# Attention and mixture of experts in one kernel: pooled value sums split 80 + 64 instead of 128 + 16, and two steps of the last slot issued earlier

## The chip, the cores and the metric

The kernel runs on one core of a Trainium2 chip. Its time is the device time of one execution in microseconds (us). The times shown are three runs and one execution under the hardware profiler.

## The reference

What is computed is attention at two scales, added up, and its rows then go through a mixture of eight experts, of which each row uses one:

```python
B, H, S, D = 8, 8, 576, 64
# q, k, v pooled: means over 4 neighbouring tokens, 144 rows in all
q_d, k_d, v_d = (t.reshape(B, H, S // 4, 4, D).mean(axis=3) for t in (q, k, v))
out_up = np.repeat(softmax(q_d @ k_d.T / 8) @ v_d, 4, axis=2)
mask = np.abs(pos[:, None] - pos[None, :]) < 4
out_local = softmax(where(mask, q @ k.T / 8, -1e9)) @ v
x = (out_up + out_local), as [4608 rows, 512]
# mixture of experts: E = 8, w1 [E, 512, 1024], w2 [E, 1024, 512]
logits = normalized(x) @ normalized(expert_emb).T / tau
e = argmax(logits)
out[row] = softmax(logits)[e] * (relu(x[row] @ w1[e]) @ w2[e])
```

## The kernel before

**Attention stage.** A unit is one batch and one pair of heads: 32 units, `for i in range(-2, n + 1)` in `attention`. The order of the operations in one round of that loop is written out by hand in `ORDER`, and `LEAD` says how many units ahead of the round each operation works. The operations that concern the change are those of the pooled attention, on 144 pooled tokens, which are cut into two pieces by the constant `CD` (line 26), because 144 is more than the 128 partitions:

- `load_v` (line 345) loads the values of one unit, one pooled token (four rows of 64 numbers, for each of two heads) in a partition. Piece 0 is one DMA, piece 1 another, both issued by SyncE (SP) into one tile `ld_v` (program name `vr`), of which there are three. `load_v(u + 3)` is called once `vd` of unit u is issued.
- `op_pv` (line 407) adds, on GpSimd (POOL), two rows of each four to the other two, once for each piece. `op_vd` (line 411) adds the two sums that are left, for both pieces in one instruction over all partitions of the tile; the rows of piece 1 that hold no token were set to zero at the start (line 246).
- `op_wdT` (line 493) transposes the pooled attention weights `ad` on TensorE (PE), three transposes for each piece, `op_adT` (line 499) copies them out of PSUM on ScalarE (ACT), and `op_vald` (line 505) multiplies them with `vd`: for each piece and head one fp32 matmul, which the trace shows as two passes. The pieces are accumulated in PSUM.

**Slot stage.** The rows are sorted by expert into slots of at most 128 rows. Three slots are handled early, 38 in `run_slots` (line 1007), and five more by a second call of `run_slots` in `last_slots` (line 1088), inside an `If` whose flag says whether there are that many; in the data used here the flag is zero and the block is skipped. For a slot q, `mm1_half` multiplies with w1 (twice 12 matmuls), `hidden_high` and `hidden_low` split the result into two fp16 parts, `hidden_T` transposes them by DMA into `hT`, and `mm2_part` multiplies with w2 (24 matmuls), which in the program's order is done one slot later, while slot q + 1 is at its first product. `out_rows` scales the result on ACT, and `store` scatters it to DRAM by an indirect DMA of POOL. The last slot has no successor: its second product, `self.mm2(last)` on line 1079, stands alone at the end.

The weights on chip belong to one expert. `renew(which, b)` (line 992) holds the steps that replace them when the expert changes, inside `If`s on a code which ACT, VectorE (DVE) and POOL have in a register. When the `If` isn't taken, the engine branches over it and then, at the line of the `If` (995), waits for its own earlier instructions and raises its semaphore by as much as the block would have. TensorE waits for these semaphores before it reads w2.

In `run_slots` the steps at the end of a slot are issued in this order: `weigh` (ACT exponential, line 1184), `out_rows(q - 1)` (ACT, line 1259), a conditional load, `gate` (DVE), `renew(1, b)`, `store(q - 1)` (POOL, line 1263). The value of the flag for the rare slots is read by `values_load` (line 1091), which puts a number into a register of each of the five engines; the branch on it is line 1092. The end of the program is line 1394.

Of the kernel before, what the change touches and what calls it, by code (L numbers as in the profile page):

```python
# [8 lines left out]
F32 = mybir.dt.float32  # L9
# [10 lines left out]
B, H, S, D = 8, 8, 576, 64  # L20
N, DM, E, FF = B * S, H * D, 8, 1024
NHP = H // 2
SD = S // 4
G, QB = S // 64, 32
WK, WV = QB + 6, 64 + 6
CD = (128, SD - 128)
CP = S // 6
TB = 128
NTB = -(-S // TB)
# [3 lines left out]
NEARLY, BEARLY = 3, B - 2  # L33
AHEAD = 4
NFIX = NSLOT - 5
# [27 lines left out]
class Kern:  # L63
# [128 lines left out]
    def attention(self, ctx):  # L192

        nc = self.nc
# [3 lines left out]
        z = self.pool(ctx, "zeroed", 1)  # L198
        self.kq, self.an, self.qdbd, self.vw, self.xT, self.sums = [], [], [], [], [], []
        for i in range(2):  # L200
# [3 lines left out]
            self.an.append(z.tile([128, G, WV], F32, name=f"an{i}"))  # L204
            self.sums.append(z.tile([128, G + 3], F32, name=f"sums{i}"))
            self.vw.append(z.tile([WV, G, 4, D], F32, name=f"vw{i}"))
        self.vr = [z.tile([128, 2, 2, 4 * D], F32, name=f"ld_v{i}") for i in range(3)]
        self.lg = z.tile([TB, NTB, E + 1], F32, name="lg")
        self.oh = self.cp.tile([TB, B, NTB + 1, E], BF16, name="oh")
        units = [(b, hp) for b in range(B) for hp in range(NHP)]  # L210
# [32 lines left out]
            nc.vector.memset(self.xT[i][:, S:], 0.0)  # L243
            nc.vector.memset(self.sums[i], 1.0)
        for vr in self.vr:
            nc.gpsimd.memset(vr[:, 1], 0.0)
        next(crows)
        load(1)
        load_v(0)
# [12 lines left out]
        for i in range(-2, n + 1):  # L262
# [4 lines left out]
            for j, (name, args) in enumerate(ops):  # L267
# [10 lines left out]
                else:  # L278
# [6 lines left out]
                    s = st[u]  # L285
# [31 lines left out]
            if i >= 1 and units[i - 1][1] == NHP - 1:  # L317
                for f in tail:
                    f()
                b = units[i - 1][0]  # L320
# [88 lines left out]
        self.nc.gpsimd.tensor_tensor(out=vr[:, :, 0:2 * D], in0=vr[:, :, 0:2 * D], in1=vr[:, :, 2 * D:], op=ALU.add)  # L409

    def op_vd(self, s):
        v, vd = s["v"], self.wk.tile([128, 2, 2, D], F32, name="vd")
        s["vd"] = vd
        self.nc.gpsimd.tensor_tensor(out=vd, in0=v[:, :, :, 0:D], in1=v[:, :, :, D:2 * D], op=ALU.add)

# [82 lines left out]

    def op_adT(self, s, c):
        if "adT" not in s:  # L500
            s["adT"] = self.wk.tile([128, 2, 2, 3, 48], F32, name="adT", bufs=1)
        self.nc.scalar.activation(out=s["adT"][:CD[c], c].rearrange("p h c j -> p c h j"),
                                  in_=s["wdT", c].rearrange("p c (h j) -> p c h j", h=2), func=AF.Copy)

# [499 lines left out]
        with tc.If(code > 4 if which else code < 1):  # L1004
            self.measure(which)

    def run_slots(self, q0, q1):

        last = q1 - 1
        for q in range(q0, q1):  # L1010
            b = q - NEARLY
            old, new, ahead = q > q0, q < last, q + 2 < q1
            first = self.mm1_half(q, 0)
            self.total(slice(0, 2))
            second = self.mm1_half(q, 1)
            if old:
                self.scale_gate(q - 1)
            self.scales(slice(0, 2))
            h2 = self.hidden_high(first)
            self.hidden_low(first, h2)  # L1020
            if not b:
                self.flags(1)
            self.nc.vector.tensor_copy(out=self.wcur, in_=self.wold)
            if new:
                self.renew(0, b + 1)
            if ahead:
                self.x_square(q + 2)
            h3 = self.hidden_high(second)
            if new:
                self.measure_staged(0, b + 1)  # L1030
            if ahead:
                self.x_power(q + 2)
            if b:
                self.measure_staged(1, b)
            ps, done = None, 0
            if old or not b:
                ps, done = (None, 0) if b else (self.begun, 4)
                ps = self.mm2_part(q - 1, done, done + 1, ps)
                done += 1
            if not b:  # L1040
                for _ in self.late:
                    pass
            if ahead:
                self.x_high(q + 2)
            if b + 2 < q1 - NEARLY:
                self.flags(b + 2)
            self.logits(q, False)
            self.hidden_T(q, 0, h2)
            if q + 4 < q1:
                self.gather(q + 4)  # L1050
            if ps:
                self.mm2_part(q - 1, done, 4 if b else 6, ps)
            if new:
                self.stage_next(0, b + 1, 0)
            self.hidden_low(second, h3)
            if ps:
                self.mm2_part(q - 1, 4 if b else 6, 8, ps)
            self.hidden_T(q, 1, h3)
            if ahead:
                self.x_low(q + 2)  # L1060
            self.weigh(q)
            if ahead:
                self.turn(q + 2)
            if ps:
                self.out_rows(q - 1, ps)
            if q > q0 + 1:
                self.stage_next(1, b - 1, 1)
            self.gate(q)
            if old:
                self.renew(1, b)  # L1070
            if new:
                self.norms(q + 1)
                self.stage_next(0, b + 1, 1)
            if ps:
                self.store(q - 1)
            if old:
                self.stage_next(1, b, *((0,) if new else (0, 1)))
        self.scale_gate(last)
        self.mm2(last)
        self.store(last)  # L1080

# [6 lines left out]
    def last_slots(self):  # L1088

        q0, q1 = NEARLY + NFIX, NEARLY + NSLOT  # L1090
        more = self.nc.values_load(self.flg[:1, NFIX, 3:4], min_val=0, max_val=1)  # L1091
        with self.tc.If(more > 0):
            for q in range(q0, min(q0 + 4, q1)):
                self.gather(q)
            for b in (NFIX, NFIX + 1):
                self.flags(b)
            self.rescale()
            for w in range(2):
                self.renew(w, NFIX)
                if not w:  # L1100
                    self.nc.vector.tensor_copy(out=self.wcur, in_=self.wold)
                    self.measure_staged(0, NFIX)
                self.stage_next(w, NFIX, 0, 1)
            self.open_slots(q0)
            self.run_slots(q0, q1)
# [161 lines left out]
    def run(self):  # L1267
        tc, ctx = self.tc, self.ctx
        ctx.enter_context(tc.manual_schedule())
        self.bk = self.pool(ctx, "banks", 8, space=PSUM)  # L1270
        self.cp = self.pool(ctx, "const", 1)
        self.dr = self.pool(ctx, "scratch", 1, space=DRAM)
        self.weight_tiles()
        self.slot_pools()
        n = B * NHP
        with ExitStack() as actx:
            w0 = self.first_weights()
            steps = self.attention(actx)
            early = self.early_slots()
            for at in steps:  # L1280
                if at is None:
                    break
                if at in EARLY:
                    next(early)
                i, end = at
                if end and i in W0:
                    next(w0, None)
                if at == (n - 1, 1):
                    ps = [self.mm1_half(0, 0, 0, 1)]
                if at == (n, 1):  # L1290
                    self.mm1_half(0, 0, 1, 3, ps[0])

            next(steps)
            self.mm1_half(0, 0, 3, 4, ps[0])
            ps.append(self.mm1_half(0, 1, 0, 2))
            next(steps)
            for _ in steps:
                pass
        self.hd = self.pool(ctx, "hidden", 2)
        self.hidden(0, 0, ps[0])  # L1300
        self.mm1_half(0, 1, 2, 4, ps[1])
        self.sw = self.pool(ctx, "slots", 1)
        slots = self.slots()
        next(slots)
        self.hidden(0, 1, ps[1])
        w1 = self.second_weights()
        for _ in range(2):
            next(w1)
        next(slots)
        self.hidden(1, 0, self.mm1_half(1, 0))  # L1310
        next(w1)
        self.hidden(1, 1, self.mm1_half(1, 1))
        next(w1)
        ps = self.mm1_half(2, 0)
        next(slots)
        self.gather(NEARLY)
        self.hidden(2, 0, ps)
        next(w1)
        self.gates(0)
        for q in range(1, AHEAD):  # L1320
            self.gather(NEARLY + q)
        ps = self.mm2_part(0)
        self.out_rows(0, ps)
        self.store(0)
        self.x_size(NEARLY)
        ps = self.mm1_half(2, 1)
        self.x_split(NEARLY)
        self.hidden(2, 1, ps)
        next(w1)
        self.gates(1)  # L1330
        self.x_size(NEARLY + 1)
        self.norms(NEARLY)
        ps = self.mm2_part(1)
        self.x_split(NEARLY + 1)
        next(w1)
        self.out_rows(1, ps)
        self.store(1)
        next(slots)
        self.begun = self.mm2_part(2, 0, 4)
        self.gates(2)  # L1340
        for _ in range(3):
            next(w1)
        for _ in self.slot_flags():
            pass

        def late():
            next(slots)
            yield from w1

        self.late = late()  # L1350
        self.run_slots(NEARLY, NEARLY + NFIX)
        self.last_slots()


# [43 lines left out]
```

## Time and profile before

| | us |
|---|---|
| three runs | 730.84, 736.08, 740.85 |
| their median | 736.08 |
| the profiled execution | 733.08 |
| its span, first to last instruction | 731.4 |
| busy in it: PE, DVE, ACT, POOL | 701.0, 473.1, 462.0, 443.4 |

The profiled execution is one of the faster ones. Its span ends 1.7 us short of its own time. Durations and instants below are counted from the start of that span. In the profile, a row of a group has the line, engine, operation, names, shapes and count, then total busy time and the mean in ns of one, then idle time before it and what ended that idle time.

### The profile page before, as it was taken

The numbers are of one execution on the slowest core, as the hardware profiler recorded it, in microseconds if no ns is written. First come the engines' busy times: TensorE is split into PE (matmuls) and PEld (weight loads), VectorE is DVE, ScalarE is ACT, GpSimd is POOL, SyncE is SP. The second block draws the span as 40 slices with busy tenths as digits, with TensorE's granted clock in tenths as the row PEclk, the third lists the DMA queues.
The fourth block names the chain that finished last, engine by engine and source line by source line (L and its number), as shares of the span: only waits on it lengthen the run. The fifth ranks groups of instructions, "written<-read, shape, count | busy, mean of one in ns | idle before, by whom it ended". The sixth has DMA issues, their size and how long they took to land. (4 is left out here: it accounts for less than half of the span.)

```text
span 731.4 us, 22049 instructions
## 1 busy us (share of the span) xinstructions
PE 701.0 (96%) x7471; PEld 412.9 (56%) x7471; DVE 473.1 (65%) x1415; ACT 462.0 (63%) x1063; POOL 443.4 (61%) x857
## 2 busy tenths in 40 slices
PE   8999999989999989999999999999999999999992
PEld 5777887768878864444444444444444444444440
DVE  6778799958998887576556467565643565366320
ACT  4677788667787664356666577775755555558420
POOL 5865788765878885556564564556466645564420
PEclk9999999989999999999999999999999999999997
DMA  9889889988788976959959988898897599779640
GB/s 162 163 202 193 221 185 234 211 210 213 158 215 185 215 244 129 221 123 248 235 126 250 231 208 216 191 247 193 251 220 132 116 238 216 147 175 202 177 74 19
DMA packets 284117, 138.92 MB, mean 190 GB/s; under 512 B 251186, under 2 KB 260402, under 8 KB 283968
## 3 DMA queue, kind: packets, MB, share of 16 engines
q1 hardware_dynamic: 277248, 118.15, 73.8%
q0 software_dynamic: 6560, 19.03, 8.2%
q8 instruction: 61, 1.00, 0.6%
q14 instruction: 88, 0.72, 0.3%
q10 hardware_dynamic: 160, 0.02, 0.0%
HBM read 213.05 MB, written 20.33 MB: 319 GB/s over the span
## 5 line engine op out<-in xcount | busy, mean ns | idle before, releaser
L1214 PE MATMUL bank<-w1h,xT 128*128 128x512 f16 x328 | 124.3, 379 | 1.4 <-ACTq L995 1.4
L1250 PE MATMUL bank<-w2h,hT 128*128 128x512 f16 x328 | 124.4, 379 | 0.9 <-ACTq L995 0.9
L1215 PE MATMUL bank<-w1l,xT 128*128 128x512 f16 x328 | 124.3, 379 | 0.1
L1252 PE MATMUL bank<-w2h,hT 128*128 128x512 f16 x328 | 124.4, 379 | 0.0
L1251 PE MATMUL bank<-w2l,hT 128*128 128x512 f16 x328 | 124.4, 379 | 0.0
L1216 PE MATMUL bank<-w1h,xT 128*128 128x512 f16 x328 | 124.3, 379 | 0.0
L1111 POOL DMA_INDIRECT xg<-xd,ids x41 | 45.8, 1118 | 79.7 <-POOLq L995 36.9
L1227 ACT ACTIVATE h<-bank 128x512 f16<-128x512 f32 x82 | 48.3, 589 | 58.4 <-PE bank L1216 57.5
L1263 POOL DMA_INDIRECT out_dram<-o,ids x41 | 44.9, 1096 | 50.0 <-ACTq L995 20.0
L380 ACT ACTIVATE kq<-bank 128x288 f32<-128x288 f32 x128 | 48.1, 472 | 38.8 <-PE bank L373 38.4
L833 ACT ACTIVATE junk<-st 128x1024 bf16<-128x1024 f32 (+1 forms) x30 | 67.5, 2251 | 4.6 <-DVE end L734 2.7
L1259 ACT ACTIVATE o<-bank,gt 128x512 f32<-128x512 f32 x41 | 27.8, 677 | 63.5 <-issue 18.7
L409 POOL TENSOR_TENSOR ld_v<-ld_v 128x256 f32<-128x256 f32 x64 | 48.9, 783 | 22.6 <-DMA ld_v<-in_v_dram 22.6
L389 POOL TENSOR_TENSOR pool_kq<-kq 128x288 f32<-128x288 f32 x62 | 45.3, 731 | 25.1 <-ACT kq L380 25.1
L81 POOL TENSOR_SCALAR nw_t<-nw_y,nw_a 128x1 f32<-128x1 f32 x123 | 51.7, 420 | 12.4
L1231 DVE SCALAR_TENSOR_TENSOR h<-bank,h 128x512 f16<-128x512 f32 x82 | 56.3, 688 | 2.7 <-ACTq L1004 2.2
L858 DVE SCALAR_TENSOR_TENSOR w2l<-st,wscl,w2h 128x1024 f16<-128x1024 f32 x32 | 39.6, 1280 | 26.1 <-ACT w2h L857 26.1
L1214 PEld LDWEIGHTS <-xT 128*128 128x128 f16 x328 | 35.1, 107 | 34.5 <-DMA xT<-x 0.5
L1251 PEld LDWEIGHTS <-hT 128*128 128x128 f16 x328 | 32.0, 98 | 39.4 <-issue 1.2
L1250 PEld LDWEIGHTS <-hT 128*128 128x128 f16 x328 | 32.0, 98 | 39.0 <-DMA hT<-h 0.6
L1216 PEld LDWEIGHTS <-xT 128*128 128x128 f16 x328 | 31.9, 97 | 39.1 <-issue 0.4
L1252 PEld LDWEIGHTS <-hT 128*128 128x128 f16 x328 | 32.0, 98 | 38.8
(221 smaller groups left out, 1556.2 us busy)
## 6 DMA issues: line engine op xcount, KB each, us to landing
st<-in_moe_w_dram SPq DMA_DIRECT2D x148, 1024.0 KB
ld_k<-in_k_dram SPq DMA_DIRECT2D x64, 144.0 KB
ld_q<-in_q_dram SPq DMA_DIRECT2D x64, 144.0 KB
xd<-xr SPq DMA_DIRECT2D x8, 1040.0 KB
ld_v<-in_v_dram SPq DMA_DIRECT2D x32, 256.0 KB
st<-in_moe_w_dram SPq DMA_DIRECT2D x16, 512.0 KB
vw<-in_v_dram SPq DMA_DIRECT2D x64, 122.5 KB
vw<-in_v_dram SPq DMA_DIRECT2D x32, 64.0 KB
```

The source lines that it names most:

```text
L81: g.tensor_scalar(out=t, in0=y, scalar1=y, scalar2=a, op0=ALU.mult, op1=ALU.mult)
L380: self.nc.scalar.activation(out=dst, in_=s["qk", r, w].rearrange("p (m i) -> p i m", m=3), func=AF.Copy, scale=(KSC, QSC)[w])
L409: self.nc.gpsimd.tensor_tensor(out=vr[:, :, 0:2 * D], in0=vr[:, :, 0:2 * D], in1=vr[:, :, 2 * D:], op=ALU.add)
L833: self.nc.scalar.activation(out=junk, in_=src, func=AF.Square, accum_out=acc)
L1214: nc.tensor.matmul(out=ps, lhsT=xT[:, 0, k], rhs=self.w1h[:, k, ns], start=(k == 0), stop=False)
L1215: nc.tensor.matmul(out=ps, lhsT=xT[:, 0, k], rhs=self.w1l[:, k, ns], start=False, stop=False)
L1216: nc.tensor.matmul(out=ps, lhsT=xT[:, 1, k], rhs=self.w1h[:, k, ns], start=False, stop=(k == self.KC - 1))
L1227: self.nc.scalar.activation(out=h2[:, 0], in_=ps, func=AF.Relu)
L1231: self.nc.vector.scalar_tensor_tensor(out=h2[:, 1], in0=ps, scalar=0.0, in1=h2[:, 0], op0=ALU.max, op1=ALU.subtract)
L1250: nc.tensor.matmul(out=ps, lhsT=hh, rhs=self.w2h[:, j, :], start=(j == 0), stop=False)
L1251: nc.tensor.matmul(out=ps, lhsT=hh, rhs=self.w2l[:, j, :], start=False, stop=False)
L1252: nc.tensor.matmul(out=ps, lhsT=hl, rhs=self.w2h[:, j, :], start=False, stop=(j == self.FC - 1))
```

## The change

`CD` goes from (128, 16) to (80, 64), and the tiles `ld_v`, `vd` and `adT` from 128 partitions to 80. The zeros at the start are written only to rows 64 to 79 of piece 1. In `run_slots`, the renewal of w2 for the last slot stands ahead of `out_rows(q - 1)`, a conditional load and `gate` rather than behind them; for all other slots it stays. The load of the rare slots' flag is issued after `scale_gate(last)`, ahead of `mm2(last)`, instead of after `store(last)`; the `If` on it stays where it was.

```diff
-CD = (128, SD - 128)
+CD = (80, SD - 80)
...
-        self.vr = [z.tile([128, 2, 2, 4 * D], F32, name=f"ld_v{i}") for i in range(3)]
+        self.vr = [z.tile([CD[0], 2, 2, 4 * D], F32, name=f"ld_v{i}") for i in range(3)]
...
-            nc.gpsimd.memset(vr[:, 1], 0.0)
+            nc.gpsimd.memset(vr[CD[1]:, 1], 0.0)
...
-        v, vd = s["v"], self.wk.tile([128, 2, 2, D], F32, name="vd")
+        v, vd = s["v"], self.wk.tile([CD[0], 2, 2, D], F32, name="vd")
...
-            s["adT"] = self.wk.tile([128, 2, 2, 3, 48], F32, name="adT", bufs=1)
+            s["adT"] = self.wk.tile([CD[0], 2, 2, 3, 48], F32, name="adT", bufs=1)
...
-    def run_slots(self, q0, q1):
+    def run_slots(self, q0, q1, end=None):
...
             self.weigh(q)
             if ahead:
                 self.turn(q + 2)
+            if old and not new:
+                self.renew(1, b)
             if ps:
                 self.out_rows(q - 1, ps)
             if q > q0 + 1:
                 self.stage_next(1, b - 1, 1)
             self.gate(q)
-            if old:
+            if old and new:
                 self.renew(1, b)
...
         self.scale_gate(last)
+        if end:
+            end()
         self.mm2(last)
         self.store(last)
...
-        more = self.nc.values_load(self.flg[:1, NFIX, 3:4], min_val=0, max_val=1)
-        with self.tc.If(more > 0):
+        with self.tc.If(self.more > 0):
...
-        self.run_slots(NEARLY, NEARLY + NFIX)
+
+        def more():
+            self.more = self.nc.values_load(self.flg[:1, NFIX, 3:4], min_val=0, max_val=1)
+
+        self.run_slots(NEARLY, NEARLY + NFIX, more)
```

## The prediction, made before the changed kernel was run

> **What bounds the kernel now.** First the page's head, then the windows of the two stages and of the one stretch that stands out, to see whether TensorE ever has room.
>
> ```profile
> span 731.4 us, 22049 instructions
> PE 701.0 (96%) x7471; PEld 412.9 (56%) x7471; DVE 473.1 (65%) x1415; ACT 462.0 (63%) x1063; POOL 443.4 (61%) x857
> ...
> 17.00:275.00 258.00, 249.01 (x5166) 198.69 (x5166) 215.04 (x550) 193.39 (x623) 193.27 (x312) 0.99 0.87 203
> 145.00:153.00 8.00, 5.78 (x121) 4.33 (x119) 5.42 (x16) 7.39 (x23) 5.68 (x10) 1.00 1.04 282
> 153.00:161.00 8.00, 7.48 (x128) 6.45 (x128) 3.26 (x7) 3.16 (x7) 3.28 (x6) 0.57 0.65 161
> ```
>
> A windows row gives the length, then busy us of PE, weight loads, DVE, ACT and POOL, the granted clock, the DMA engines' busy share and GB/s. PE is busy 249 of the attention stage's 258 us: it bounds that stage, and the other engines have a quarter of it free. The DMA engines, at 0.87, are the second bound, and the first in bursts: in 145 to 153 they are full and PE idles 2.2 of 8 us, and in the next 8 us its clock is granted at 0.57, so some 0.43 x 8 = 3.4 us more are lost. What the changed operations wait for in that stage, by the view of waits:
>
> ```profile
> POOL ld_v L409 <- DMA ld_v<-in_v_dram: 22.6, 10, 5.0
> PE bank L522 <- DMA vw<-in_v_dram: 3.3, 5, 2.0
> PE bank L509 <- POOL vd L414: 0.9, 1, 0.9
> ```
>
> The pooled values' loads make POOL wait ten times, 22.6 us in all, but POOL has that time: PE waited only once, 0.9 us, for `vd`. Next the end, by the timeline:
>
> ```profile
> 707.05 0.19 ACT L1184 ACTIVATION_READ_ACCUMULATOR lg<-lg,lmx 128x1 f32 x1
> 710.84 0.38 PE L1252 MATMUL bank<-w2h,hT 128*128 128x512 f16 x1
> 711.30 0.69 ACT L1259 ACTIVATE o<-bank,gt 128x512 f32<-128x512 f32 x1 [4.07 <-issue]
> 712.09 0.38 PE L1250 MATMUL bank<-w2h,hT 128*128 128x512 f16 x1 [0.87 <-ACTq L995]
> ...
> 716.83 0.38 PE L1251 MATMUL bank<-w2l,hT 128*128 128x512 f16 x1
> 717.05 0.38 PE L1252 MATMUL bank<-w2h,hT 128*128 128x512 f16 x1
> 717.60 0.69 ACT L1259 ACTIVATE o<-bank,gt 128x512 f32<-128x512 f32 x1 [5.61 <-PE bank L1252]
> 718.57 0.99 POOL L1263 DMA_INDIRECT out_dram<-o,ids  x1 [5.07 <-ACT o L1259]
> ```
>
> At 712.09 the last second product starts late, and L995, the `If` of `renew`, is what it waited for. Matmuls follow each other by 0.22 us (716.83, 717.05), so the lateness is 712.09 - 710.84 - 0.22 = 1.03 us. This is the whole of PE's idle time at the end, and everything behind it (output copy, store) follows PE.
>
> **The change part by part. The renewal.** The rows of line 995 in the last 32 us:
>
> ```profile
> L995 ACTq COMPARE_BRANCH  x2: 45/45/45, 700.8 to 711.3; - x2
> L995 ACTq EVENT_SEMAPHORE  x2: 17/17/17, 701.5 to 712.0; - x2
> ...
> L995 DVEq EVENT_SEMAPHORE  x1: 21/21/21, 707.8 to 707.8; - x1
> ```
>
> The `If` isn't taken, so the renewal is a branch of 45 ns and one semaphore event, for which ACT first finishes what it has issued. ACT's branch stands behind the output copy of the slot before, which waits for PE until 711.30 and ends at 711.99; the event comes at 712.0, and PE starts at 712.09. Ahead of the copy, the event follows `weigh`, which ends at 707.24: about 707.3, almost 4 us before PE wants it. DVE's event is at 707.8 already; with `gate` behind it nothing of it is later than that by more than the two events' 0.1 us, and `gate` is wanted only by the copy at 717. What is late next is the transpose into `hT`:
>
> ```profile
> L1238 SPq DMA_TRANSPOSE hT<-h x2: 1232/1232/1232, 704.8 to 707.5; - x2
> ...
> L1250 PEld LDWEIGHTS <-hT 128*128 128x128 f16 x328 | 32.0, 98 | 39.0 <-DMA hT<-h 0.6
> ```
>
> The halves are issued until 706.0 and 708.7; the first is wanted at 711.06 and the second 12 matmuls later, at 713.6, 5 us behind each issue, and in 328 weight loads of that line PE has waited 0.6 us for such a transpose. So PE starts at 711.06: 1.03 us less. The conditional loads of SP behind the renewal come earlier too; their condition is off in the last slot (no slot follows), and nothing waits for them but the program's end.
>
> **The flag's load.** The rows of lines 1091 and 1092:
>
> ```profile
> L1091 PEldq EVENT_SEMAPHORE  x6: 51/51/51, 713.4 to 713.9; - x6
> ...
> L1091 PEldq TENSOR_LOAD <-flg x1: 564/564/564, 714.1 to 714.1; - x1
> L1091 ACTq TENSOR_LOAD <-flg x1: 275/275/275, 717.6 to 717.6; - x1
> L1091 POOLq TENSOR_LOAD <-flg x1: 287/287/287, 718.3 to 718.3; - x1
> ...
> L1092 POOLq EVENT_SEMAPHORE  x6: 17/30/43, 721.4 to 721.8; - x6
> ...
> L1092 POOLq COMPARE_BRANCH  x1: 45/45/45, 718.7 to 718.7; - x1
> L1092 POOLq INC_SWDGE_SEM  x1: 1820/1820/1820, 721.9 to 721.9; - x1
> ...
> out_dram<-o,ids POOLq DMA_INDIRECT x2, 3.0
> L1394 POOLq DRAIN  x3: 46/107/6772, 723.8 to 731.1; - x3
> ```
>
> POOL sets the end: the load of the flag at 718.3, the branch at 718.7, 2.7 us until the first instruction behind the skipped block (721.4), six events, 1.82 us, a drain of 6.77 us, and the end at 731.4. The load stands in that chain, ahead of the branch, for 0.29 us. Moved ahead of `mm2(last)` it falls into POOL's idle time before the store, so with the renewal the branch comes 1.03 + 0.29 earlier, at 717.4, and the sixth event at 720.5. There the store's landing is late next: 3.0 us from issue by the median of the two, so at 717.54 + 3.0 = 720.54, where 720.5 was wanted. The two together give 1.03 + 0.29 - 0.04 = 1.28 us, if the 1.82 and 6.77 us stay what they are. On ACT the load goes from beside the copy to its wait for PE. On PE the six events and the load, 1.2 us of its sequencer (713.4 to 714.64), now stand ahead of the matmuls. Before, they ran while matmuls went on without a gap, 3.4 us ahead of the last of them in the program, so the sequencer leads PE by more than they take. I cost them at nothing; without that lead they cost up to 1.2 us, in place of the 1.03.
>
> **80 and 64.** The rows of each changed operation, its shapes kept apart, and of the loads:
>
> ```profile
> L409 POOL TENSOR_TENSOR ld_v<-ld_v 128x256 f32<-128x256 f32 x32 | 25.2, 788 | 22.1 <-DMA ld_v<-in_v_dram 22.1
> L409 POOL TENSOR_TENSOR ld_v<-ld_v 16x256 f32<-16x256 f32 x32 | 24.9, 779 | 0.5 <-DMA ld_v<-in_v_dram 0.5
> L509 PE MATMUL bank<-adT,vd 128*64 128x144 f32 x128 | 14.9, 311 | 1.5 <-POOL vd L414 0.9 <-ACT adT L502 0.6
> L509 PE MATMUL bank<-adT,vd 16*64 16x144 f32 x128 | 14.8, 307 | 0.0
> L496 PE MATMUL bank<-ident,ad 96*16 96x96 f32 x96 | 13.2, 245 | 0.9 <-DVE ad L478 0.8
> L496 PE MATMUL bank<-ident,ad 96*128 96x96 f32 x96 | 13.1, 246 | 0.0
> L502 ACT ACTIVATE adT<-bank 16x288 f32<-16x288 f32 x32 | 12.8, 399 | 15.7 <-PE bank L496 15.7
> L502 ACT ACTIVATE adT<-bank 128x288 f32<-128x288 f32 x32 | 12.2, 383 | 0.0
> ld_v<-in_v_dram SPq DMA_DIRECT2D x32, 256.0 KB
> ld_v<-in_v_dram SPq DMA_DIRECT2D x32, 32.0 KB
> ```
>
> Between 16 and 128 partitions POOL's sum changes by 9 ns, PE's matmul by 4, its transpose by 1, ACT's copy by 16 (16 partitions the slower). 80 and 64 lie between, in the same number of instructions with the same row lengths: nothing, with bounds of 32 x 50 ns = 1.6 us on either side, if PE took a 64-row matmul otherwise than a 16-row one. The zeros at the start are as long in each row as before; nothing. The loads move 288 KB a unit as before, in two DMAs, but as 160 and 128 KB. At the stage's 203 GB/s the first piece lands 96 KB or 0.47 us earlier and the second when it did; the first sum takes 0.79 us, so the second hardly waits, and `vd` is done some 0.3 us sooner where POOL waited. PE waited for `vd` once: -0.3 us, bounds -0.9 and 0.
>
> Sum: -1.28 - 0.3 = -1.6 us, from 733.08 to 731.5 in the profiled execution. The median of the runs is 3.0 above that execution, so as a median: 736.08 - 1.6 = **734.5 us**. The three runs lie within 10 us, 1.4%; so 2% is about what a measurement of this kernel can tell from no change, and this is far below.
>
> **The rivals.** [...]
>
> [...]
>
> (b) *The end doesn't move:* PE's sequencer has no lead, as it may stand at a wait until 710.8, and its 1.2 us replace the 1.03; POOL's 0.25 remain: 736.08 + 0.2 - 0.25 - 0.3 = 735.7. Against: the lead of 3.4 us above.
>
> (c) *Faster:* with the first piece landing sooner and the bursts shifted, the stretch from 145 to 161 goes: 2.2 + 3.4 = 5.6 us more, 729. For it: such a stretch is luck of the DMA queue. Against: the bytes are the same.
>
> **How the numbers follow.** The forecast 0.62, (a) 0.12, (b) 0.16, (c) 0.10. The forecast's own range is that of the runs, 730 to 739.5. The range reaches to (c) and half of the way into (a): 728.5 to 741. Over 2% faster would be below 721.4, which no case gives: 0.02; over 2% slower is above 750.8, the far part of (a): 0.03; within, 0.95.
>
> **What the profile would show.** ACT's event of line 995 near 707.3, no gap of PE ahead of the last product, its flag load before that product, POOL's branch right behind the store, and the end 1.3 us nearer to the last but one product; `ld_v` waits of POOL near 22 us, rows of lines 409, 496, 502 and 509 unchanged within 20 ns. What would make it wrong: a DMA share above 0.9 in the attention stage and longer waits for `vw`, which is (a), or a gap before the last product with PE's line 1091 in it, which is (b).

## The result and the profile after

The changed kernel took 739.76 us in the median of 20 runs (734.30 to 745.55), the kernel before 734.38 us of 20 on the same chip. The ratio is 1.0063 with a 95% interval of 1.0042 to 1.0084: it is slower by some 4.6 us, where 1.6 us less had been forecast. The change is below 2%, and 739.76 lies inside the range, but on the wrong side of before. The profiled execution took 741.49 us, its span 739.7.

The head of the page and the windows of the kernel after, their columns as in the prediction (length, busy us of PE, weight loads, DVE, ACT and POOL, granted clock, DMA share, GB/s):

```profile
span 739.7 us, 22045 instructions
PE 706.7 (96%) x7471; PEld 418.1 (57%) x7471; DVE 471.5 (64%) x1415; ACT 463.5 (63%) x1063; POOL 444.1 (60%) x857
```

```profile
17.00:275.00 258.00, 246.86 (x5049) 198.52 (x5047) 204.81 (x512) 187.05 (x598) 187.23 (x296) 0.97 0.88 198
60.00:72.00 12.00, 10.24 (x180) 7.82 (x179) 7.58 (x19) 7.91 (x28) 6.07 (x11) 0.86 1.08 185
137.00:145.00 8.00, 6.63 (x133) 5.24 (x131) 4.47 (x12) 3.92 (x14) 3.49 (x5) 0.74 0.96 190
161.00:169.00 8.00, 7.76 (x110) 6.58 (x111) 4.71 (x11) 3.88 (x9) 7.03 (x11) 0.57 0.97 199
```

In the same 258 us the loads moved 198 GB/s instead of 203 at a DMA share that is higher, 0.88 for 0.87. All of the loss lies in the attention stage: the last unit's mask product (line 418) stands at 270.7 us instead of 261.0. Up to there PE was busy for 257.0 us instead of 251.2, with 5089 matmuls in both, and idle for 13.7 instead of 9.8: more than half of these 9.7 us are matmuls that took longer, not waits. Before had one stretch at a low clock (0.57, 153 to 161 us); now there are three inside the stage. The number of such stretches in one execution is no sign of the split, though: the kernel with the end alone, below, whose attention stage is that of before, shows three as well (0.57 in 73 to 77 and in 138 to 142 us, 0.51 in 155 to 162).

What the changed operations take and wait for, shapes kept apart, and the waits for loads in the attention stage, both of the kernel after; then the two of these waits of the kernel before that the prediction doesn't show:

```profile
L409 POOL TENSOR_TENSOR ld_v<-ld_v 80x256 f32<-80x256 f32 x32 | 25.6, 798 | 21.7 <-DMA ld_v<-in_v_dram 21.7
L409 POOL TENSOR_TENSOR ld_v<-ld_v 64x256 f32<-64x256 f32 x32 | 25.5, 798 | 0.9 <-DMA ld_v<-in_v_dram 0.9
L509 PE MATMUL bank<-adT,vd 80*64 80x144 f32 x128 | 15.0, 311 | 1.2 <-ACT adT L502 0.6 <-POOL vd L414 0.6
L509 PE MATMUL bank<-adT,vd 64*64 64x144 f32 x128 | 14.8, 308 | 0.0
L502 ACT ACTIVATE adT<-bank 64x288 f32<-64x288 f32 x32 | 12.9, 403 | 15.8 <-PE bank L496 15.8
```

```profile
POOL ld_v L409 <- DMA ld_v<-in_v_dram: 22.6, 8, 5.9
PEld bank L522 <- DMA vw<-in_v_dram: 4.2, 8, 0.9
PE bank L522 <- DMA vw<-in_v_dram: 2.9, 5, 0.8
PE bank L373 <- DMA ld_q<-in_q_dram: 2.6, 2, 1.8
```

```profile
PEld bank L522 <- DMA vw<-in_v_dram: 1.9, 4, 0.6
PE bank L373 <- DMA ld_q<-in_q_dram: 0.4, 1, 0.4
```

Every row of an operation is where the prediction put it, within 20 ns (the transposes of line 496, not shown, at 245 and 246), and POOL waits for the value rows no longer than before, 22.6 us. What grew are TensorE's waits for loads that the change doesn't touch: its weight loads waited 4.2 us for `vw` where they had waited 1.9, and PE waited 2.6 us for `ld_q` where it had waited 0.4. Only PE's own waits for `vw` are much as they were, 2.9 us for 3.3. These rows of single executions don't say where the loss comes from: of the kernels below, the one with the end alone, which isn't slower, has 3.7 us in the first of them, and the one with the split alone, which is, has 0.2 us in the second.

The end, by the rows of its lines (line numbers are 3 to 7 higher now, and the load of the flag stands on line 1356) and by the last second product's groups:

```profile
L995 ACTq EVENT_SEMAPHORE  x3: 17/17/17, 703.2 to 716.9; - x3
...
L1356 PEldq EVENT_SEMAPHORE  x6: 51/51/51, 717.5 to 718.1; - x6
L1356 PEldq TENSOR_LOAD <-flg x1: 867/867/867, 718.2 to 718.2; - x1
...
L1095 POOLq COMPARE_BRANCH  x1: 45/45/45, 727.0 to 727.0; - x1
```

```profile
L1253 PE MATMUL bank<-w2h,hT 128*128 128x512 f16 x24 | 9.1, 379 | 0.0
```

The group is of the last slots: no idle time is left ahead of the second product's first line, where before had 0.9 us behind line 995. PE's flag load stands at 718.2 us, 7.5 us ahead of the last matmul at 725.69, and no matmul waits for it. That matmul is now 14.0 us from the end of the span; before it was 14.3 (717.05 to 731.4). The end does what was forecast: PE's gap of 1.03 us is gone, and the end is 0.3 us nearer to the last matmul.

### The profile page after: what moved, and what is told of

Its sections match the earlier page's. It is cut to its first block, busy times and chain, and to the rows that moved or that the text cites. A ratio compares the mean times of both kernels' runs of the same rounds, so it can differ in the third digit from the quotient of the medians.

```text
span 739.7 us, 22045 instructions
## 1 busy us (share of the span) xinstructions
PE 706.7 (96%) x7471; PEld 418.1 (57%) x7471; DVE 471.5 (64%) x1415; ACT 463.5 (63%) x1063; POOL 444.1 (60%) x857
## 5 line engine op out<-in xcount | busy, mean ns | idle before, releaser
L409 POOL TENSOR_TENSOR ld_v<-ld_v 80x256 f32<-80x256 f32 x64 | 49.9, 798 | 22.6 <-DMA ld_v<-in_v_dram 22.6
L81 POOL TENSOR_SCALAR nw_t<-nw_y,nw_a 128x1 f32<-128x1 f32 x123 | 54.2, 440 | 12.4
L491 ACT ACTIVATE aT<-bank 70x384 f32<-70x384 f32 x96 | 43.5, 486 | 19.6 <-PE bank L484 16.0
L1253 PEld LDWEIGHTS <-hT 128*128 128x128 f16 x328 | 32.1, 98 | 39.2 <-DMA hT<-h 1.1
L1255 PEld LDWEIGHTS <-hT 128*128 128x128 f16 x328 | 32.1, 98 | 38.7
```

What stands on the lines that cost most here:

```text
L81: g.tensor_scalar(out=t, in0=y, scalar1=y, scalar2=a, op0=ALU.mult, op1=ALU.mult)
L1253: nc.tensor.matmul(out=ps, lhsT=hh, rhs=self.w2h[:, j, :], start=(j == 0), stop=False)
L1255: nc.tensor.matmul(out=ps, lhsT=hl, rhs=self.w2h[:, j, :], start=False, stop=(j == self.FC - 1))
```

## The experiments

Theories at the start: the split's loads are slow (A, by the partitions they go to), the operations' shapes cost PE (B), any edit loses by chance (C), the end costs (D). Ratios are to the kernel before on the same chip, with 95% intervals.

**The end alone.** Against the changed kernel: the edit puts the split back; the changes at the end stay.

```diff
-CD = (80, SD - 80)
+CD = (128, SD - 128)
```

> The two changes at the end alone (renewal and flag's load moved); the pooled sums stay at 128 and 16 tokens. Theory A (the split's loads are slower: a unit's transfer took 1.69 us before and 2.13 after by the packets' records, and PE's waits for DMAs and the half-clock stretches behind them are what was lost): the attention stage is as before (its last mask product near 261 us, not 271) and the end 1.3 us shorter, ratio to before 0.998, some 733 us. Theory B (the matmuls' shapes cost PE): the same, 0.998. Theory C (any edit shifts the queue of DMAs and the loss is chance): anything from 0.993 to 1.007. Theory D (the changes at the end cost): 1.005 or more.

Measured: 734.45 us, ratio 1.0006 (0.9978 to 1.0034). D, which gave 1.005 or more, falls. The 1.3 us of the end are too few to be seen in this interval; they are seen in the trace only.

**The split alone.** The kernel before with the split's five lines and nothing at the end.

```diff
-CD = (128, SD - 128)
+CD = (80, SD - 80)
```

> The split into 80 and 64 tokens alone, the end as before. Theory A (slower loads): the whole loss and the 1.3 us that the end had given back, ratio 1.008, some 740.5 us, with the packets of these loads near 60 ns in the mean instead of 56 and more time at half clock in the attention stage. Theory B (matmul shapes): the same 1.008. Theory C (chance): the same program as the changed kernel in that stage, so 1.008 again, unless the chance is per execution. Theory D (the end costs): 1.000.

Measured: 740.79 us, ratio 1.0113 (1.0068 to 1.0159). The whole loss is in the split.

**The 64 rows in the upper partitions.** The second piece goes to partitions 64 to 127; its transposes are 128 columns wide to get there.

```diff
+RD = (slice(0, 80), slice(64, 128))
...
-            self.nc.sync.dma_start(out=vr[:n, c], in_=...)
+            self.nc.sync.dma_start(out=vr[RD[c], c], in_=...)
```

> The split alone, but the 64 tokens of the second piece lie in partitions 64 to 127 instead of 0 to 63; the products have the same 80 and 64 rows, the DMAs the same number and bytes. Theory A in its form by partitions (the loads crowd into the lower 64 partitions): like before or a little better, ratio 0.997 to 1.002, the packets near 56 ns. Theory B (shapes of the products, or the split of the bytes between the two DMAs): like the split, 1.008. Theory C (chance of the schedule): anywhere between 0.995 and 1.010. [...]

Measured: 741.98 us, ratio 1.0113 (1.0078 to 1.0149), as with the lower partitions. That the loads crowd into partitions 0 to 63, which was the rival (a) of the prediction and theory A, is not what this loss comes from.

**112 and 32.**

```diff
-CD = (128, SD - 128)
+CD = (112, SD - 112)
```

> Another split, 112 and 32 tokens, the end as before. Theory A by partitions: 112 rows reach nearly as many partitions above 64 as 128 do, so the loads take as long as before (packets near 56 ns) and the ratio is 0.998 to 1.002. Theory B (other shapes than 128 and 16 cost PE): 1.003 to 1.008. Theory C (any edit may lose by chance): 0.995 to 1.010. [...]

Measured: 736.77 us, ratio 1.0039 (1.0013 to 1.0064). A smaller loss, in the range that B gave, with an interval that reaches into A's. So loads and operations had to be taken apart.

**Operations without the loads, loads without the operations.** One pair of sizes for the loads, another for all else; the first kernel computes on 80 and 64 rows, the second loads 80 and 64.

```diff
-CD = (128, SD - 128)
+CD, LD = (80, SD - 80), (128, SD - 128)   # operations alone
+CD, LD = (128, SD - 128), (80, SD - 80)   # loads alone
...
-        for c, n in enumerate(CD):
+        for c, n in enumerate(LD):
```

> Loads as before (128 and 16 rows), but all operations on 80 and 64 rows, with 48 rows of each piece left out of or added to the sums as zeros: the result lacks the tokens of rows 80 to 127. Theory L (the loads of two pieces of similar size are what is slow, whatever partitions they go to: second piece 1.03 us in the median from its first packet to its last, against 0.40 before): like before, 0.998 to 1.003. Theory B (the operations' shapes cost, on PE, or by their power on the granted clock): like the split, 1.009 to 1.013. Theory C (any edit here loses some us by chance of the schedule): 1.003 to 1.010 here and in the counterpart as well.

> The counterpart: loads of 80 and 64 rows, but all operations on 128 and 16 rows as before; rows 80 to 127 of the first piece are zeros and 48 rows of the second are not used, so the result lacks tokens. Theory L (loads of similar size are slow): 1.008 to 1.013, packets near 60 ns. Theory B (the operations' shapes): 0.998 to 1.003. Theory C (any edit): 1.003 to 1.010.

Measured: operations alone 735.58 us, 1.0006 (0.9976 to 1.0036); loads alone 741.97 us, 1.0086 (1.0058 to 1.0114). B falls. C is unlikely: an edit that changed the shapes of all these operations cost nothing. The loads carry the loss, some 6 us.

**More DMAs for the same rows.** The 128 rows as two halves by partitions, or as two heads over all partitions; then the 16 rows.

```diff
+        for c, p0, n, t0 in ((0, 0, 64, 0), (0, 64, 64, 256), (1, 0, 16, 512)):   # halves
+            self.nc.sync.dma_start(out=vr[p0:p0 + n, c], in_=...)
...
+        for i in range(2):                                                          # heads
+            self.nc.sync.dma_start(out=vr[:, 0, i], in_=...)
```

> The operations as before, the 128 rows loaded by two DMAs of 64 partitions each, then the 16 rows: three DMAs a unit. Theory A by partitions, what is left of it: the first half's DMA crowds into the lower partitions, slower than the control with the same number of DMAs by 3 us or more. Theory L in the form that an additional DMA of some size is what costs: 1.005 to 1.012 here and in the control alike. Theory B (shapes of the operations): 0.998 to 1.003 in both.

> The control of the halves: the operations as before, the 128 rows loaded by two DMAs of one head each over all 128 partitions, then the 16 rows: three DMAs a unit. Theory A by partitions: like before, 0.998 to 1.003, and 3 us or more faster than the halves. Theory L in the form that an additional DMA costs: 1.005 to 1.012, as the halves. Theory B: 0.998 to 1.003.

Measured: halves 755.51 us, 1.0268 (1.0237 to 1.0299); heads 739.19 us, 1.0059 (1.0031 to 1.0086). Both lose, with the operations of before, and the halves by 16 us more than the control with the same number of DMAs. Theory A had the halves slower than the heads, but the run with the upper partitions speaks against its reason; L fits the heads, and no theory gave as much as the halves lost. The rows of the load's line say where the difference is. They are of the kernel before, the kernel after, the halves and the heads, in this order (minimum, median and maximum ns of SP's issue):

```profile
L348 SPq DMA_DIRECT2D ld_v<-in_v_dram x62: 384/420/1821, 21.0 to 255.9; - x62
```

```profile
L348 SPq DMA_DIRECT2D ld_v<-in_v_dram x62: 317/602/1568, 20.4 to 258.6; - x62
```

```profile
L348 SPq DMA_DIRECT2D ld_v<-in_v_dram x93: 542/601/1622, 19.5 to 279.6; - x93
```

```profile
L348 SPq DMA_DIRECT2D ld_v<-in_v_dram x62: 328/422/1897, 19.4 to 261.0; - x62
L350 SPq DMA_DIRECT2D ld_v<-in_v_dram x31: 327/422/1419, 20.4 to 261.5; - x31
```

SP takes 0.42 us to issue a load of 128 or 16 rows, and 0.60 us where 64 rows are among them. A load of 64 rows also makes the next issue longer: in the halves no issue took less than 0.542 us, though a third of them are of 16 rows, and in the kernel after the 80 rows took 0.549 us in the median right behind a load of 64, but 0.318 behind other loads. By these medians the halves hold SP for 93 x 0.601 - 62 x 0.420 = 30 us more than before, the heads for 93 x 0.422 - 62 x 0.420 = 13 us more. That counts only if SP has no time to spare; the timeline of SP in the kernel before shows none:

```profile
58.86 2.79 SPq L342 DMA_DIRECT2D ld_k<-in_k_dram  x2
61.69 1.30 SPq L342 DMA_DIRECT2D ld_q<-in_q_dram  x2
63.04 0.62 SPq L877 DMA_DIRECT2D st<-in_moe_w_dram  x1
63.76 1.11 SPq L357 DMA_DIRECT2D vw<-in_v_dram  x2
64.92 3.92 SPq L363 DMA_DIRECT2D vw<-in_v_dram  x4
68.93 1.20 SPq L357 DMA_DIRECT2D vw<-in_v_dram  x2
70.22 1.89 SPq L348 DMA_DIRECT2D ld_v<-in_v_dram  x4
```

Each row's start and length reach to the next row's start within 0.1 us. By the issues' own records SP is in an issue, or in the gap of under 0.15 us behind one, for 241 of the 247.5 us from 17.2 to 264.7 in the run with the end alone. If so, what one load takes longer to issue, every later load of keys, queries and windows is late by. A filled queue isn't proof of a bound, as it may itself be held up: in the kernel before, 44 of 324 issues in that stretch took over 1 us, 68 us in all, and what held them isn't shown. This gave two new theories: I, SP's issue time is the cost, and P, the transfers themselves are slower.

**Loads alone, a shape at a time.** The kernel only issues loads, twelve of a shape back to back. Asked is whether a load of 64 rows is only slower to issue (I), whether it is slower to carry (P), and whether the order in which the device memory is read is what makes it slow (H):

```diff
+    for name, p0, p1, nh in SHAPES:
+        for r in range(REP):
+            nc.sync.dma_start(out=buf[p0:p1, r, :nh], in_=src)
```

> Loads alone: neither attention nor experts are computed, the output is filled with other numbers. SP issues twelve loads of the value rows of one shape back to back, then a pause, then the next shape: 128 rows x 2 pieces of 1 KB, 64 (partitions 0 to 63), 128 again, 64 (partitions 64 to 127), 80, 112, 96, 32, 16 rows x 2, 128 rows x 1, 64 rows x 2 out of the same 128 KB as the phase before, 48 x 2. [...] Theory I (such a load is only slower to issue on SP): packets of 46 to 50 ns in all phases, and an issue of 0.6 us on 64 rows, 0.32 to 0.42 on 128 and 80. Theory H (the other side, the order in which the device memory is read, makes it slow): the 64 rows out of the same 128 KB behave like the 128 x 1 rows. [...]

The rows of the issuing line in the phases of 128, 64 (lower), 64 (upper), 80 and 16 rows, each from the phase's own stretch:

```profile
L34 SPq DMA_DIRECT2D ld<-in_v_dram x12: 367/469/540, 6.4 to 12.4; - x12
L34 SPq DMA_DIRECT2D ld<-in_v_dram x12: 597/605/717, 24.1 to 31.4; - x12
L34 SPq DMA_DIRECT2D ld<-in_v_dram x12: 605/606/613, 58.5 to 65.6; - x12
L34 SPq DMA_DIRECT2D ld<-in_v_dram x12: 344/442/442, 74.3 to 79.6; - x12
L34 SPq DMA_DIRECT2D ld<-in_v_dram x12: 312/422/422, 138.2 to 143.2; - x12
```

And the windows of the phases of 128, 64 lower, 64 upper, 80, 112, 96, 128 x 1, 64 out of the same 128 KB, and 48 (length, POOL, clock, DMA share, GB/s):

```profile
6.40:18.00 11.60, 0.01 (x1) 1.00 0.84 271
24.10:33.00 8.90, 0.00 (x1) 1.00 0.59 164
58.50:67.50 9.00, 0.00 (x0) 1.00 0.59 167
74.30:84.00 9.70, 0.00 (x0) 1.00 0.85 203
90.30:103.00 12.70, 0.01 (x1) 1.00 0.81 217
108.60:119.00 10.40, 0.00 (x0) 1.00 0.87 226
150.90:159.00 8.10, 0.01 (x1) 1.00 0.67 194
164.70:174.00 9.30, 0.01 (x1) 1.00 0.58 169
180.60:189.00 8.40, 0.00 (x0) 1.00 0.83 141
```

Theory I holds for 64 rows, in whichever half: 0.605 us an issue, against 0.42 to 0.47 in all other shapes. GB/s over DMA share is what the engines move while they are busy: 271 / 0.84 = 323 GB/s on 128 rows (244 / 0.82 = 298 in their second phase, from 40.1 to 53.0 us), 278 and 283 on 64, and 291 on 64 out of the same 128 KB, the same as the 290 of its counterpart of 128 x 1. So 64 rows are slow to issue and little slower to carry. By the packets' records a piece of 1 KB took 50 and 55 ns in the two phases of 128 rows and 57 in both of 64, above the 46 to 50 of I. But 80 rows give 239, 112 give 268, 96 give 260 and 48 give 170: there the transfer itself is slower. These phases weren't equally full, so the rates are of the shapes as issued here: the engines were busy for 0.81 to 0.87 of the time in these four, for 0.59 in those of 64 rows. Theory H doesn't explain the long issue, 0.606 us on 64 rows and 0.430 on 128 x 1 of the same memory; in the transfer the two do behave alike, as H expected, and equally fast.

**One more issue, with 64 bytes.**

```diff
+        self.nc.sync.dma_start(out=self.tiny, in_=self.v[b, 2 * hp, :1, :16])
```

> The kernel before with one more load a unit on SP, of 64 bytes that nothing uses: 32 more issues of some 0.4 us, 13 us in a queue that was issuing or between issues for 241 of the first 247 us of the attention stage in the profile of the changes at the end alone. Theory I (SP's queue of issues is the bound behind PE): 1.004 to 1.012. Theory P (only the transfers count): 0.998 to 1.002.

Measured: 741.79 us, ratio 1.0115 (1.0065 to 1.0164): 8.5 us for 64 bytes a unit. The issue's row, and the wait of SP that the load brought with it:

```profile
L351 SPq DMA_DIRECT2D tiny<-in_v_dram x31: 242/270/282, 21.2 to 264.0; - x31
```

```profile
SPq L351 <- DMA tiny<-in_v_dram: 4.4, 8, 0.8
```

The issues are 31 x 0.27 = 8.4 us, and SP waited 4.4 us for the tile's load before: 12.8 us of SP's time cost 8.5 us. Per us of SP that is 0.66; the halves' 19.7 us for 30 give 0.66 too, the heads' 4.3 for 13 only 0.33 (the interval of the 8.5 alone is 3.6 us on either side). SP's queue is a bound of the attention stage beside PE, shown with the other transfers unchanged.

**The second load from ACT's queue.** With 128 and 16 rows, and with 80 and 64, the end changed in both:

```diff
-            self.nc.sync.dma_start(out=vr[:n, c], in_=...)
+            (self.nc.sync, self.nc.scalar)[c].dma_start(out=vr[:n, c], in_=...)
```

> The changes at the end with the loads of 128 and 16 rows, the one of 16 rows issued by ACT instead of SP: 32 issues of 0.46 us, 15 us, leave SP's queue, and some 15 to 20 us come to ACT, which is busy 193 of 258 us in the attention stage. Theory I: faster than the kernel before, 0.985 to 0.995. Theory P: as with the changes at the end alone, 0.998 to 1.001. Slower (1.005 or more) if ACT stands at the issue while PE waits for its copies.

> The changed kernel (80 and 64 rows, the changes at the end) with the load of 64 rows issued by ACT instead of SP: 32 issues of 0.61 us, 20 us, leave SP's queue. Theory I: the loss of the split is gone, 0.985 to 0.997, as with the 16 rows issued by ACT or a little less. Theory P: the loss stays, 1.005 to 1.010. Both: between, with the difference to the 16 rows issued by ACT as the share of P.

Measured: 772.93 us, 1.0513 (1.0454 to 1.0572), and 784.01 us, 1.0682 (1.0617 to 1.0746). Both theories missed, and the third case of the first expectation came, as ACT stood. The first row of ACT's waits in the kernel with 16 rows:

```profile
ACT xr L551 <- POOL vd L414: 43.1, 8, 7.5
```

The load has to wait for its buffer, which POOL's `vd` frees, and everything that ACT has behind it waits along; in the kernel before ACT has no wait for `vd` in that stage. The runs say nothing on SP's share.

**More shapes alone.**

```diff
+    ("e64", 3, 67, 4), ("e60", 3, 63, 4), ..., ("r64", 0, 64, 2), ("r60", 0, 60, 2), ("r72", 0, 72, 2), ...
```

> Loads alone again, without attention and experts, twelve of a shape back to back: the window's edges with 4 pieces of 256 bytes a row on 64, 60, 56, 48, 3, 7 and 11 rows, then the value rows with 2 pieces of 1 KB on 64, 60 and 72 rows, then 4 pieces of 1 KB on 128 and on 16 rows. Theory I in the form that 64 rows are an exception: 0.60 to 0.64 us of issue on 64 rows in both kinds, 0.40 to 0.45 on 60, 56 and 48. In the form that the issue grows with the pieces: a smooth row without a step at 64.

The rows of the edge loads on 64 and 60 rows, then of the value rows on 64 and 60:

```profile
L30 SPq DMA_DIRECT2D ld<-in_v_dram x12: 590/612/752, 11.6 to 18.9; - x12
L30 SPq DMA_DIRECT2D ld<-in_v_dram x12: 382/436/437, 32.5 to 37.7; - x12
...
L35 SPq DMA_DIRECT2D ld<-in_v_dram x12: 605/605/670, 136.2 to 143.4; - x12
L35 SPq DMA_DIRECT2D ld<-in_v_dram x12: 332/417/418, 157.2 to 162.2; - x12
```

64 rows are an exception and not the upper end of a slope: 0.61 us with 256 pieces of 256 bytes and 0.605 with 128 of 1 KB, while 60 rows take 0.44 and 0.42. In the transfer 60 rows are the slower ones, 168 / 0.75 = 224 GB/s against 161 / 0.56 = 288.

**Slower transfer without the long issue: 96 and 48, 84 and 60.**

```diff
-CD = (128, SD - 128)
+CD = (96, SD - 96)   # and (84, SD - 84)
```

> The split into 96 and 48 tokens, the end as before. Theory I alone (SP's issue time is the whole cost): 0.31 to 0.45 and 0.43 us a unit, no more than the 0.39 and 0.46 of before, so 0.996 to 1.001. Theory P (slower packets cost as much or more): 62 and 94 ns instead of 50 and 58 are some 0.3 to 0.4 us of all 16 engines a unit, 10 to 12 us in the stage, so 1.004 to 1.012. Both, in the split of 80 and 64: here 1.002 to 1.005, as in 112 and 32 (1.0039).

> The split into 84 and 60 tokens, the end as before. Theory I alone (the 64 rows' issue is the whole cost): 0.996 to 1.001. Theory P alone: like 80 and 64, 1.008 or more. Both: like 96 and 48 and like 112 and 32, 1.003 to 1.006, with packets of 60 ns or more.

Measured: 739.55 us, 1.0056 (1.0021 to 1.0090), and 740.23 us, 1.0060 (1.0033 to 1.0087). The issue's row and the stage's window of 84 and 60:

```profile
L348 SPq DMA_DIRECT2D ld_v<-in_v_dram x62: 317/401/1597, 20.3 to 259.0; - x62
```

```profile
17.00:265.00 248.00, 236.48 (x4876) 189.89 (x4873) 197.00 (x493) 181.52 (x577) 178.25 (x280) 0.96 0.93 194
```

The same stretch of the kernel before:

```profile
17.00:265.00 248.00, 240.44 (x5049) 192.96 (x5048) 207.10 (x515) 185.46 (x598) 185.31 (x291) 0.99 0.88 205
```

The issue of 84 and 60 is quicker than before (0.401 for 0.420), yet the time is 4.4 us longer. In the profiled execution (745.57 us, one of its slower ones) the DMA engines are busy for 0.93 of the stage, not 0.88, and carry 194 GB/s, not 205. By elimination the cost in these splits is the transfer's, so P seems to hold in this form beside I. It is argued and not shown: no run changed the transfer alone, the higher share by itself need not cost (the fastest version, below, has 0.92), and the crowding of the lower partitions was tested with 64 rows only. How much each theory has in 80 and 64 the two intervals don't tell.

**SP's time taken away.** The edge loads of the windows were of 64 and 3 rows; cut as 60 and 7, on top of the changes at the end alone:

```diff
-            for i, n in ((0, 64), (64, WV - 67)):
+            for i, n in ((0, 60), (60, WV - 63)):
```

> The changes at the end, loads of 128 and 16 rows, and the window's edge loads cut as 60 and 7 rows instead of 64 and 3: the same bytes and number of DMAs. In the phases alone 60 and 7 rows were issued in 0.436 and 0.301 us, 64 and 3 in 0.612 and 0.276: 0.15 us less a pair, 64 pairs in the stage, 9.7 us less on SP. Theory I (SP's issue time counts, by the tiny load's 8.5 us of time for some 10 us of issues, and the halves' 20 for 31): 5 to 8 us faster, on top of what the end gives, ratio 0.988 to 0.996. Theory P alone (only the packets count; those of 256 bytes took 17.6 ns in all shapes): as with the changes at the end alone, 0.998 to 1.003.

Measured: 732.47 us, ratio 0.9946 (0.9917 to 0.9976): 4.0 us less than before, with the same bytes and number of DMAs. The row of the edge loads, of this kernel; the kernel before had a median of 591 ns there (both edges' loads together):

```profile
L357 SPq DMA_DIRECT2D vw<-in_v_dram x64: 274/418/2201, 13.0 to 248.7; - x64
```

The expected 5 to 8 us were too many: they count 64 pairs of edge loads, but the row has 64 loads, 32 pairs. By the phases alone that is 32 x 0.15 = 4.8 us less on SP, not 9.7. Of the 4.0 us the end may have its 1.3; the other 2.7 are 0.56 for each of the 4.8, between the 0.33 and 0.66 above. Theory P alone is out, as it gave 0.998 to 1.003. This is the fastest of the versions run, and the only one that beats the kernel before.

## Why the prediction was wrong, point by point

**The step that failed** is "80 and 64", of the sum's second term. It was given -0.3 us, with bounds of -0.9 and 0 for the loads; it cost 6 to 8 us (loads alone 6.3, the split alone 8.3, with intervals of 2.1 and 3.4 us on either side). The operations were costed at nothing from rows of 16 and 128 partitions, rightly: alone they gave 1.0006. The loads were costed by bytes, "in two DMAs as before" at the stage's 203 GB/s. Two prices of a DMA that do not follow its bytes were left out, and a third item may stand behind both:

- *The issue.* SP's queue in the attention stage has no term in the sum, though one timeline of it shows the stage filled. By the issues' records, each piece by itself, the medians were 0.389 and 0.458 us a unit before and 0.480 and 0.614 after: 0.25 us more a unit, 8 us in 32; at the 0.33 to 0.66 us that a us of SP cost in the runs above, 2.6 to 5.2 us, an estimate.
- *The transfer.* By the packets' records a piece of 1 KB took 55.8 ns before and 60.2 after, and a unit's transfer, first packet to last, 1.69 us before and 2.13 after in the median, in which the later start of the second load is contained. "The second when it did" was thus off by 0.4 us a unit. Splits of 112, 96 and 84 rows, whose issues are no longer than before in the median, lost 2.9 to 4.4 us; in 84 and 60 a unit's transfer took 2.16 us.
- *The clock.* The mean granted clock of the executions fell in most of the slower kernels: by the medians to 0.9735 from 0.983 in the split alone, to 0.976 from 0.982 with the loads alone, to 0.967 from 0.982 in the halves, but only to 0.982 from 0.983 in 84 and 60. Of a span of some 738 us, 0.0095 is 7.0 us at full clock and 0.006 is 4.4, estimates of what matmuls can have lost by it. Late loads may thus cost through the clock as well as by waits; whether they bring the low clock about was not tested.

The first two together are 5.5 to 9.6 us, if they add, and cover what was measured. How they divide the loss of 80 and 64 stays open: 84 and 60 (1.0060) against 80 and 64 (1.0113) would show the issue's part, but their intervals overlap, and the transfers differ as well.

**Rival (a)**, loads of 64 rows slowed by the partitions they go to, gave 745 us: the right sign and place, and about twice the size (8.9 us more given, 4.6 measured). That it came so near is luck. It priced a load of 64 rows at 101 GB/s instead of 203, and no run shows that rate or that cause, on which the range's upper end of 741 rests too: loads into the upper partitions cost the same (1.0113 in both), and alone 64 rows moved 164 and 167 GB/s over their phases. A rate above some 198 GB/s, 128 KB for each 0.66 us from one start to the next, couldn't show there, as SP issued no faster; what 64 rows reach where more is asked was not measured. 128 rows of two pieces were the quickest to carry, 298 and 323 GB/s while the engines were busy, against 170 to 291 in the other shapes; why isn't shown. The second sum's wait of 0.5 us behind a load of 16 rows says nothing against slow loads: POOL has slack (busy for 193 of 258 us), and its waits for `ld_v` were 22.6 us before and after.

What should have shown (a), a DMA share above 0.9 and longer waits for `vw`, came out as 0.88, and as longer waits of the weight loads only. Neither sign parts the slower kernels from the others: the kernel with the end alone has 3.7 us of that wait, and the fastest one a share of 0.92.

**The end** came as forecast, in the trace: the gap ahead of the last second product is gone (1.03), and the end is 0.3 us nearer to the last matmul. ACT's event of line 995 stands 8.8 us ahead of the last matmul (716.9 and 725.69); by the forecast these were 707.3 and 716.02, 8.7 us. PE's flag load took 0.87 us, not 0.56, and its sequencer had the lead that rival (b) doubted. As a time the gain is within the interval of its own run (1.0006, 0.9978 to 1.0034).

**Rival (c)**, bursts shifted to fewer stretches at a low clock, didn't come: the windows above have three instead of one, as the kernel with the end alone has.

**Smaller readings that were off.** The 3.4 us of lead of PE's sequencer are 3.6 by the prediction's own rows, from 713.4 to 717.05, and 2.4 from the end of the load; either is more than the 1.2 that were needed. DVE had a sixth of the attention stage free (215 of 258 us busy), not a quarter. The 50 ns in the bounds of the operations had no row behind them; no operation changed by more than 19.

## What to carry to other kernels

Where loads come close behind one another, read the queue that issues them as an engine: lay its timeline out, and if it has no gaps, price every edit of a load by its issue time as well as by its transfer. To see whether the queue is a bound, add one tiny load to each unit (here 64 bytes, 8.5 us in 32 units). Take a DMA's price from a row of the same count or measure the shape alone: here 64 rows took 0.605 us to issue and were carried at 278 to 291 GB/s, where 60 and 80 rows took 0.42 and 0.44 us and 224 and 239 GB/s, so neither price lay between its neighbours. Moving the load of 16 rows to ACT's queue moved its wait for a buffer there as well (43.1 us, 8 waits for `vd`).

## What the runs showed of the hardware

- 64 rows took SP 0.605 to 0.612 us to issue, in two kinds of load and in either half of the partitions; 16, 32, 48, 60, 80, 96, 112 and 128 rows took 0.42 to 0.47. The issue behind a load of 64 rows was longer too (0.549 us instead of 0.318 on 80 rows). Why isn't shown. It isn't the only long issue: the loads of keys and queries took 0.63 us.
- While busy, the DMA engines moved pieces of 1 KB at 298 and 323 GB/s into 128 rows (290 with one piece a row), at 278 to 291 into 64, at 239 to 268 into 80, 96 and 112, at 224 into 60 and at 170 into 48.
- A load of 64 bytes, issued in 0.27 us, cost 8.5 us in 32 units (4.8 to 12.1), as much as the whole split.
